# Splitting the late row blocks of a spectral-filter and GEGLU kernel into rounded halves, with three products each

## The chip, the core and the metric

The kernel runs on one core of a Trainium2 chip. A core has five engines that work in parallel, each through its own queue of instructions in a fixed order: PE (TensorE, matrix products into PSUM), ACT (ScalarE), DVE (VectorE), POOL (GpSimd) and SP (SyncE, which here only issues transfers). They wait for one another on semaphores. SBUF is the working memory, PSUM has eight banks of 128x512 floats for the products. The metric is the device time of one execution in microseconds; three runs gave 454.14, 454.15 and 454.22.

## What is computed

Two residual stages on x of 2048 rows by 512 columns, each behind a layer norm without weights (`_layernorm`): a filter in the two-dimensional Fourier domain, then a gated feed-forward.

```python
h = x + irfft2(rfft2(_layernorm(x)) * (w_r + 1j * w_i))
n = _layernorm(h)
h2 = h + (gelu(n @ w_gate) * (n @ w_up)) @ w_down
```

w_r and w_i are 2048x257, w_gate and w_up 512x1376, w_down 1376x512.

## The kernel before

The 2048 rows are 16 row blocks of 128 (row 16p + b belongs to block b, partition p). The array `gh` holds all blocks, 128x512 each, in the residual stream's place. The Fourier stages are matrix products with constant tables; the last of them, over rows, is one product per block: `mis[:, b]` (128x128) by `gh[:, b]` (128x512), into a PSUM bank. To it the input x, read again from memory into a `row` buffer, is added, and the block's mean is taken off (L972); then the block's statistics for the second norm are taken (L514, L516).

Eight blocks (0 to 7, "first half") are finished before the feed-forward starts, by a list written out by hand (`FIRST`), which fixes the order of PE, ACT, DVE and POOL. The other eight (8 to 15, the "late" blocks) are finished while the feed-forward of the first half runs, by the generator `late(b)` (L961): unfolding by four additions and subtractions on POOL (`unfolded`, L818 to L821, done within `FIRST` for blocks 8, 9 and 12, the list `BY_THEN`), then the transfer of x, the product (L971), the residual (L972) and the statistics.

The feed-forward runs over tiles (q, f): q is the half of the rows (1024 rows as 512 columns of two halves), f one of 11 column blocks of 128 of the hidden width. A tile n has seven groups P0 to P6 of two times three matmuls (a two-by-two product by seven), accumulated in three of six PSUM banks (three for even n, three for odd n). Every product of these is done in rounded precision: each operand is split into a rounded high part and the rounded rest (type F32R), and `mm3` (L100, L101, L102) adds high by high, high by low and low by high. The product at L971 is not: there both operands are full F32.

Between the groups stand copies of the bank (c1, c2, c3: L660 on ACT), additions (d1, d2, dy: L663 on DVE), the gelu (G0, G1: L666 on ACT), the multiplication (m0, m1: L669 on DVE) and the split of the result (i: L675 on ACT, o: L682 on DVE). P2 accumulates into the bank that c1 reads, P4 into the one that c2 reads, P5 into the one that c3 reads, so PE waits for these copies. The first two tiles are done in halves within `FIRST`; the last of their splits are the steps `g1bi1` and `g1bo1`.

A tile's gate and up weights come by two transfers into the one buffer `raw` (L131, L132), are combined on POOL (L138 to L146), rounded on DVE (L153, the cast) and the rest taken on POOL (L156, three instructions). The buffer `gus` of the results has two places; the cast waits until PE has done with the tile before last.

The down products (`down`, L756) of two or three finished tiles go row block by row block into banks 6 and 7 in turn (`bank_67`), and DVE adds the bank to `gh` (L762, the eviction). The late blocks' products take their bank from the same cycle. So each down waits until the bank's last user, two places before it, has been evicted. The down weights are split by L503 (ACT) and L505 (POOL).

The loop at L993 fixes PE's order alone (`manual_schedule` with PE); the scheduler orders ACT, DVE and POOL. Per tile n it calls `step(n)` (one part of the tile: P1, then P2, P3, P4, P5, P6; P0 of the next tile comes ahead of P5) and, between them, `fill(2)` (two downs). `ending` holds the late blocks of this tile: blocks 8 and 12 for n = 2, then 9 and 13 for n = 3, 10, 14, 11, 15 for n = 4 to 7. Their products stand behind P2 (`for g in ending: next(g)`, L1008).

Of the kernel before, what the change touches and what calls it, by code (L numbers as in the profile page):

```python
# [12 lines left out]
F32 = mybir.dt.float32  # L13
F32R = mybir.dt.float32r
I32 = mybir.dt.int32
AF = mybir.ActivationFunctionType
ALU = mybir.AluOpType
PSUM = bass.MemoryType.PSUM

S, D, F = 2048, 512, 1376  # L20
P = 128
# [36 lines left out]
def kernel(  # L58
# [15 lines left out]
    nc = tc.nc  # L74
    pe, act, dve, pool = nc.tensor, nc.scalar, nc.vector, nc.gpsimd
# [4 lines left out]
    gh = base.tile([P, NB, D], F32, name="gh")  # L80
# [15 lines left out]
    def mm3(o, pairs, onto=False):  # L96

        n = len(pairs)
        for i, ((lh, ll), (rh, rl)) in enumerate(pairs):
            pe.matmul(o, lh, rh, start=(i == 0 and not onto), stop=False, skip_group_check=True)  # L100
            pe.matmul(o, lh, rl, start=False, stop=False, skip_group_check=True)  # L101
            last = pe.matmul(o, ll, rh, start=False, stop=(i == n - 1), skip_group_check=True)  # L102
        return last
# [6 lines left out]
    mis = k3.tile([P, NB, P], F32, name="mis")  # L110
# [12 lines left out]
    def held(k):  # L123

        return tc.issue_after(pooled[k].ins) if k in pooled else ExitStack()
# [369 lines left out]
    w3 = ctx.enter_context(tc.tile_pool(name="w3", bufs=2, reuse_waits="tile"))  # L495
# [12 lines left out]
    def row():  # L508
        return rp.tile([P, D], F32, name="row")
# [109 lines left out]
    def products(n, i=slice(0, 4)):  # L619

        w, at = gu[tiles[n][1]], slice(i.start * P, i.stop * P)

        x, y, z = places = [ps[:, 3 * (n % 2) + k, at] for k in range(3)]

        def product(o, wm, m, onto=False):
            def do():
                mm3(
                    o,
                    [
                        (  # L630
                            (w[:, 0, wm, c], w[:, 1, wm, c]),
                            tuple(cb[:, h, m, c, i].rearrange("p i n -> p (i n)") for h in range(2)),
                        )
                        for c in range(2)
                    ],
                    onto,
                )

            return do

        return places, {
            "P0": product(x, 0, 0),
            "P1": product(y, 1, 1),
            "P2": product(x, 2, 4, True),
            "P3": product(z, 3, 3),
            "P4": product(x, 4, 5, True),
            "P5": product(x, 5, 6, True),
            "P6": product(z, 6, 2, True),
        }

    def tile_of(n, i=slice(0, 4)):

        at = slice(i.start * P, i.stop * P)
        (x, y, z), by_pe = products(n, i)
        if n not in sums:
            sums[n] = sum_tiles()
        s1, u2, u3 = (t[:, at] for t in sums[n])

        def copy(to, a):
            return lambda: act.activation(to, a, AF.Copy)  # L660

        def add(to, a, b):
            return lambda: dve.tensor_tensor(to, a, b, op=ALU.add)  # L663

        def gelu(g):
            return lambda: act.activation(g, g, AF.Gelu_apprx_tanh)  # L666

        def times(u, g):
            return lambda: dve.tensor_tensor(u, u, g, op=ALU.mult)  # L669

        def high(k, u):
            def do():
                if n not in parts_of:
                    parts_of[n] = w3.tile([P, 2, 2, 512], F32R, name="a", bufs=3)
                act.activation(parts_of[n][:, 0, k, at], u, AF.Copy)  # L675

            return do

        def low(k, u):
            def do():  # L680
                a = parts_of[n][:, :, k, at]
                dve.tensor_tensor(a[:, 1], u, a[:, 0].bitcast(F32), op=ALU.subtract)  # L682

            return do

        return by_pe | {
            "c1": copy(s1, x),
            "d1": add(s1, y, s1),
            "c2": copy(u2, x),
            "c3": copy(u3, x),  # L690
            "dy": add(y, z, u3),
            "G0": gelu(s1),
            "m0": times(x, s1),
            "i0": high(0, x),
            "o0": low(0, x),
            "d2": add(u2, z, u2),
            "G1": gelu(u2),
            "m1": times(y, u2),
            "i1": high(1, y),
            "o1": low(1, y),  # L700
        }
# [79 lines left out]
    begun_tiles, wds, parts_of, hns, copied, sums = {}, {}, {}, {}, {}, {}  # L781
    bank_67 = itertools.cycle((6, 7))

    def sum_tiles():
        return [w3.tile([P, 512], F32, name=f"s{k}") for k in range(1, 4)]
# [10 lines left out]
    do = {}  # L796
# [17 lines left out]
    def unfolded(b, v):  # L814

        s4, v4 = (a.rearrange("p (e h n) -> p e h n", e=2, h=2) for a in (gh[:, b], v))
        u = gh[:, b].rearrange("p (e n) -> p e n", e=2)
        pool.tensor_tensor(v4[:, :, 0], s4[:, :, 0], s4[:, :, 1], op=ALU.add)  # L818
        pool.tensor_tensor(v4[:, :, 1], s4[:, :, 0], s4[:, :, 1], op=ALU.subtract)
        pool.tensor_tensor(u[:, 0], v[:, :256], v[:, 256:], op=ALU.add)  # L820
        pooled["late"] = pool.tensor_tensor(u[:, 1], v[:, :256], v[:, 256:], op=ALU.subtract)  # L821
# [121 lines left out]
    def step(n):  # L943

        if n not in begun_tiles:
            f = tiles[n][1]
            if f not in gu:
                for _ in load_gu(f):
                    pass
            begun_tiles[n] = gate_up(n)  # L950
        next(begun_tiles[n])

    do["g2P0"] = lambda: step(2)
    et = mybir.EngineType
    with tc.manual_schedule(engines={et.PE, et.Activation, et.DVE, et.Pool}):
        for op in FIRST.split():
            name, *place = op.split(".")
            do[name](*map(int, place))


    def late(b):  # L961

        if b not in BY_THEN:

            with held("lo"):
                unfolded(b, row())
        yield
        xt = row()
        nc.sync.dma_start(xt, x3[:, b])
        py = ps[:, next(bank_67)]  # L970
        pe.matmul(py, mis[:, b], gh[:, b], start=True, stop=True)  # L971
        dve.scalar_tensor_tensor(gh[:, b], xt, mv[:, b, 0:1], py, op0=ALU.subtract, op1=ALU.add)  # L972
        for _ in stats2(b):
            pass
        yield

    def normed(b):

        hn = row()
        act.activation(hn, gh[:, b], AF.Copy, scale=rs2[:, b : b + 1])  # L980
        return hn

    def fill(n):
        for _ in range(n):
            next(downs, None)
# [3 lines left out]
    ending = [late(b) for b in BY_THEN[:2]]  # L989
# [3 lines left out]
    with tc.manual_schedule(engines={et.PE}):  # L993
        for n, (q, f) in list(enumerate(tiles))[2:]:
            k, at_change = n - q * NF, n == NF - 1
            if k == 0:
                step(n)
            step(n)
            if k > 8 and not q:
                for i in range(2 * k - 18, 2 * k - 16):  # L1000
                    with tc.issue_after(copied[n - 1].ins):
                        hns[i] = [normed(b) for b in (8 + i, 12 + i)]
            step(n)
            if at_change:

                steps = [in_turn(i, hns[i], banks) for i, banks in enumerate(((3, 4), (5, 0), (3, 4), (1, 2)))]
                next(steps[0])
            for g in ending:  # L1008
                next(g)
            if n in (6, 7):  # L1010

                norm_scales(2 * n - 4, 2)
            fill(2)
            step(n)
            fill(2)
            step(n)
            fill(2)

            if k == NF - 1:
                downs = down(q, orders[q][-3:], True)  # L1020
            if at_change:
                next(steps[0])
                next(steps[1])
            elif k < NF - 1:
                step(n + 1)
                fill(2)
            else:
                fill(1)
            ending = [late(b) for b in lates.get(n, ())]
            for g in ending:  # L1030
                next(g)
            step(n)
            step(n)
            if k in (4, 7):
                downs = down(q, orders[q][: k + 1][-3:], False)
            elif k == 1:
                downs = down(q, orders[q][:2], False)
            if at_change:
                gu = {f: gu[f] for f in orders[0][-2:]}
                for s in steps:  # L1040
                    for _ in s:
                        pass
                    fill(2)
            if k == NF - 1:
                fill(12)
# [125 lines left out]
```

## Time and profile before

| what | value |
|---|---|
| median of three runs | 454.15 us (454.14 to 454.22) |
| the profiled execution's own time | 454.05 us |
| its span (first to last instruction) | 452.3 us |
| mean granted PE clock | 0.998 |
| stage of the late blocks' products | 130.7 to 213 us |

The profile is one execution. A row of a timeline is start, duration, engine, line, operation, output<-inputs, sizes, count and, in brackets, how long the engine had been idle and who released it. Matmul rows overlap, since matmuls are pipelined: the distance from start to start is what one costs. A row of the chain of waits is start, length and what it was. PEld is the weight load, which runs beside PE.

### The profile page before, as it was taken

To read this page: it belongs to the slowest core of one execution; us is meant where nothing else is said; L and a number is where in the kernel's file an instruction comes from. 1 tells how busy PE (TensorE), PEld (TensorE's weight loads), DVE (VectorE), ACT (ScalarE), POOL (GpSimd) and SP (SyncE) were. 2 spreads that over 40 slices of the span, in tenths; PEclk is the share of its full clock that TensorE was granted. 3 is DMA by queue.
4 is the path that set the end of the run, shared out by engine and by line. 5 is a ranking of instruction groups with operands and counts; after the bars stand their busy time and mean duration, and the time that the engine had idled before them with its cause. 6 is when DMAs were issued, how large, how long until landed. Compare 5 with 4: busy or idle time off the path is not lost.

```text
span 452.3 us, 6433 instructions
## 1 busy us (share of the span) xinstructions
PE 437.8 (97%) x2289; PEld 371.1 (82%) x2289; DVE 277.1 (61%) x514; ACT 205.6 (45%) x433; POOL 276.5 (61%) x306
## 2 busy tenths in 40 slices
PE   3999999999999999999999999999999999999996
PEld 3999999798878777877888888888888888888875
DVE  5957895797574766358735578266555345635453
ACT  4979785688731242033332765252243034303420
POOL 6986896878859578748662543165566636653210
PEclk9999999999999999999999999999999999999999
DMA  8994805200032022112210213121022102210013
GB/s 288 390 400 147 278 13 179 100 23 1 25 116 93 26 69 93 48 46 71 70 48 23 70 48 116 49 91 46 26 70 71 46 24 71 70 46 25 23 70 118
DMA packets 21168, 41.05 MB, mean 91 GB/s; under 512 B 2064, under 2 KB 7696, under 8 KB 21008
## 3 DMA queue, kind: packets, MB, share of 16 engines
q1 hardware_dynamic: 20992, 40.51, 26.3%
q8 instruction: 18, 0.29, 0.3%
q10 hardware_dynamic: 144, 0.13, 0.1%
q14 instruction: 14, 0.11, 0.1%
HBM read 36.44 MB, written 4.19 MB: 90 GB/s over the span
## 4 chain that ended last, share of the span: by engine, by line
PE 90%; DVE 3%; ACT 2%; DMA 2%; POOL 1%; issue 1%; SPq 0%; POOLq 0%; DVEq 0%
PE ps L756 26%; PE ps L100 15%; PE ps L102 14%; PE ps L101 14%; PE ps L288 4%; PE ps L416 3%; PE ps L427 3%; PE ps L454 3%; PE ps L524 3%; PE ps L862 1%; PE ps L971 1%; DMA gh<-in_x 1%; POOL gu L156 1%; PE ps L563 1%; DMA raw<-in_wgu 1%; PE ps L557 1%
## 5 line engine op out<-in xcount | busy, mean ns | idle before, releaser
L100 PE MATMUL ps<-cb,gu 128*128 128x512 f32 (+1 forms) x336 | 127.9, 381 | 2.0 <-ACT s L660 1.6
L756 PE MATMUL ps<-wd,a 128*128 128x512 f32 (+1 forms) x537 | 125.9, 388 | 0.2 <-DVE gh L759 0.2
L102 PE MATMUL ps<-cb,gu 128*128 128x512 f32 (+1 forms) x336 | 125.0, 372 | 0.0
L101 PE MATMUL ps<-cb,gu 128*128 128x512 f32 (+1 forms) x336 | 124.9, 372 | 0.0
L756 PEld LDWEIGHTS ps<-wd,a 128*128 128x128 f32 x537 | 99.4, 188 | 21.9 <-DVE gh L972 1.0
L156 POOL TENSOR_TENSOR gu<-raw,gu 128x768 fp32r<-128x768 f32 (+1 forms) x54 | 78.3, 1479 | 39.6 <-DVE gu L153 33.4
L660 ACT ACTIVATE s<-ps 128x512 f32<-128x512 f32 (+1 forms) x72 | 40.4, 560 | 133.8 <-PE ps L102 133.5
L100 PEld LDWEIGHTS ps<-cb,gu 128*128 128x128 f32 x336 | 63.3, 188 | 14.9 <-ACT s L660 2.2
L101 PEld LDWEIGHTS ps<-cb,gu 128*128 128x128 f32 x336 | 63.3, 188 | 11.7 <-issue 1.0
L102 PEld LDWEIGHTS ps<-cb,gu 128*128 128x128 f32 x336 | 63.3, 188 | 11.0
L762 DVE TENSOR_TENSOR gh<-ps,gh 128x512 f32<-128x512 f32 x48 | 33.1, 691 | 53.7 <-PE ps L756 53.5
L505 POOL TENSOR_TENSOR wd<-wdr,wd 128x512 fp32r<-128x512 f32 x22 | 28.4, 1291 | 51.3 <-ACT wd L503 51.2
L669 DVE TENSOR_TENSOR ps<-ps,s 128x512 f32<-128x512 f32 (+1 forms) x48 | 31.0, 650 | 24.4 <-PE ps L102 22.2
L675 ACT ACTIVATE a<-ps 128x512 fp32r<-128x512 f32 (+1 forms) x48 | 26.9, 561 | 39.0 <-DVE ps L669 38.6
L682 DVE TENSOR_TENSOR a<-ps,a 128x512 fp32r<-128x512 f32 (+1 forms) x48 | 30.8, 641 | 11.5 <-ACT a L675 9.8
L663 DVE TENSOR_TENSOR s<-ps,s 128x512 f32<-128x512 f32 (+1 forms) x48 | 30.9, 643 | 10.6 <-PE ps L102 9.1
L666 ACT ACTIVATE s<-s 128x512 f32<-128x512 f32 (+1 forms) x48 | 28.2, 592 | 18.4 <-DVE s L663 18.4
L138 POOL TENSOR_TENSOR raw<-raw 128x256 f32<-128x256 f32 x20 | 14.7, 737 | 33.9 <-DMA raw<-in_wgu 32.4
L663 DVE TENSOR_TENSOR ps<-ps,s 128x512 f32<-128x512 f32 (+1 forms) x24 | 15.7, 654 | 27.8 <-ACT s L660 27.8
L288 PE MATMUL ps<-ms,pn 128*128 128x128 f32 x120 | 17.0, 291 | 7.9 <-ACT ms L256 7.8
L288 PEld LDWEIGHTS ps<-ms,pn 128*128 128x128 f32 x120 | 15.6, 205 | 8.3 <-POOL pn L263 7.2
L153 DVE CAST gu<-raw 128x1792 fp32r<-128x1792 f32 x18 | 19.6, 1091 | 3.8 <-PE ps L101 2.9
(126 smaller groups left out, 609.5 us busy)
## 6 DMA issues: line engine op xcount, KB each, us to landing
raw<-in_wgu SPq DMA_DIRECT2D x40, 256.0 KB, 3.1
wt<-in_w SPq DMA_DIRECT2D x16, 520.0 KB, 5.7
wdr<-in_wd SPq DMA_DIRECT2D x22, 256.0 KB, 2.7
out<-gh SPq DMA_DIRECT2D x15, 256.0 KB, 2.0
gh<-in_x SPq DMA_DIRECT2D x7, 512.0 KB, 8.1
row<-in_x SPq DMA_DIRECT2D x12, 256.0 KB, 3.0
mis<-in_mi SPq DMA_DIRECT2D x1, 1024.0 KB, 10.6
a<-in_x SPq DMA_DIRECT2D x4, 256.0 KB, 4.9
```

The costliest lines, as they stand in the source:

```text
L100: pe.matmul(o, lh, rh, start=(i == 0 and not onto), stop=False, skip_group_check=True)
L101: pe.matmul(o, lh, rl, start=False, stop=False, skip_group_check=True)
L102: last = pe.matmul(o, ll, rh, start=False, stop=(i == n - 1), skip_group_check=True)
L156: pooled["lo"] = pool.tensor_tensor(r[:, 1, m], t[:, m], r[:, 0, m].bitcast(F32), op=ALU.subtract)
L288: pe.matmul(pt[:, c], o, mc, start=(z == 0), stop=(z == len(parts[b][c]) - 1))
L505: pool.tensor_tensor(r[:, 1], t, r[:, 0].bitcast(F32), op=ALU.subtract)
L660: return lambda: act.activation(to, a, AF.Copy)
L663: return lambda: dve.tensor_tensor(to, a, b, op=ALU.add)
L669: return lambda: dve.tensor_tensor(u, u, g, op=ALU.mult)
L682: dve.tensor_tensor(a[:, 1], u, a[:, 0].bitcast(F32), op=ALU.subtract)
L756: pe.matmul(o, parts_of[tiles.index((q, f))][:, ha, i // 4, r], wds[f][:, hw, c], start=start, stop=stop)
L762: dve.tensor_tensor(gh[:, b, c], o, gh[:, b, c], op=ALU.add)
```

## The change

Four parts:

1. `late(b)` gets a stage of its own ahead of the product. It splits `mis[:, b]` into `m` (high and low, 128x128 each) and `gh[:, b]` into `v` (128x512 each): the high parts by a copy on ACT, the low ones by a subtraction on DVE. The product becomes `mm3`: three rounded matmuls in the place of one full-precision product. `m` and `v` have two buffers each in the pool `w3`, 2 x 5 KB per partition.
2. The splits of the first pair (8 and 12) are held behind the second tile's last split steps: ACT's copies behind `g1bi1`, DVE's subtractions behind `g1bo1`. For that, `high` and `low` return their instruction.
3. In the loop the splits of the tile's late blocks are called behind P1, the products behind P2 as before; but for n = 2 the products come behind P4.
4. The program is built with a DMA scratch of 4096 bytes (`dynamic_dma_scratch_size`), smaller than the default.

```diff
         def high(k, u):
             def do():
...
-                act.activation(parts_of[n][:, 0, k, at], u, AF.Copy)
+                return act.activation(parts_of[n][:, 0, k, at], u, AF.Copy)
...
-                dve.tensor_tensor(a[:, 1], u, a[:, 0].bitcast(F32), op=ALU.subtract)
+                return dve.tensor_tensor(a[:, 1], u, a[:, 0].bitcast(F32), op=ALU.subtract)
...
+        behind = []
         for op in FIRST.split():
             name, *place = op.split(".")
-            do[name](*map(int, place))
+            ins = do[name](*map(int, place))
+            if name in ("g1bi1", "g1bo1"):
+                behind.append(ins)
...
             with held("lo"):
                 unfolded(b, row())
+        yield
+        m = w3.tile([P, 2, P], F32R, name="m")
+        v = w3.tile([P, 2, D], F32R, name="v")
+        for h, l, full in ((v[:, 0], v[:, 1], gh[:, b]), (m[:, 0], m[:, 1], mis[:, b])):
+            with tc.issue_after(behind[0].ins) if behind else ExitStack():
+                act.activation(h, full, AF.Copy)
+            with tc.issue_after(behind[1].ins) if behind else ExitStack():
+                dve.tensor_tensor(l, full, h.bitcast(F32), op=ALU.subtract)
         yield
         xt = row()
         nc.sync.dma_start(xt, x3[:, b])
         py = ps[:, next(bank_67)]
-        pe.matmul(py, mis[:, b], gh[:, b], start=True, stop=True)
+        mm3(py, [((m[:, 0], m[:, 1]), (v[:, 0], v[:, 1]))])
...
             step(n)
+            for g in ending:
+                next(g)
+            behind = None
...
-            for g in ending:
-                next(g)
+            if n > 2:
+                for g in ending:
+                    next(g)
...
             step(n)
             fill(2)
             step(n)
+            if n == 2:
+                for g in ending:
+                    next(g)
             fill(2)
...
-    nc = bacc.Bacc("TRN2", target_bir_lowering=False, num_devices=1)
+    nc = bacc.Bacc("TRN2", target_bir_lowering=False, num_devices=1, dynamic_dma_scratch_size=4096)
```

In the text below v8 and m8 stand for the low-part subtractions of block 8 (L977 in the new file, whose copies are L975 and whose residual is L983), and so on; "down i" is the i-th down of the first group, "residual b" the instruction at L972.

## The prediction

> **What bounds the kernel now.** I read the page first (busy shares, then the chain that ended last), then the chain in order of time from 95 us, then a table of windows around the change, then each engine's timeline there.
>
> ```profile
> span 452.3 us, 6433 instructions
> PE 437.8 (97%) x2289; PEld 371.1 (82%) x2289; DVE 277.1 (61%) x514; ACT 205.6 (45%) x433; POOL 276.5 (61%) x306
> PE 90%; DVE 3%; ACT 2%; DMA 2%; POOL 1%; issue 1%; SPq 0%; POOLq 0%; DVEq 0%
> 130.70:135.60 4.90, 4.85 (x18) 2.94 (x17) 3.46 (x6) 0.60 (x1) 3.04 (x5) 1.00 0.24 86
> 135.60:153.30 17.70, 17.70 (x80) 14.66 (x79) 10.01 (x16) 3.46 (x6) 12.85 (x14) 1.00 0.19 62
> 153.30:216.00 62.70, 62.70 (x267) 49.77 (x266) 39.81 (x76) 19.33 (x35) 46.55 (x50) 1.00 0.20 63
> ```
>
> The window rows give the length, then PE, PEld, DVE, ACT, POOL busy, granted clock and DMA. All that the change touches lies between 130.7 and 216 us. There PE is never idle, at full granted clock, so a microsecond of matmul saved is a microsecond of time, and so is each one in which PE is made to wait. DVE (39.81 of 62.70) and ACT (19.33) have room on average; POOL is busy for 12.85 of 17.70 and 46.55 of 62.70.
>
> **The products: what they cost and will cost.**
>
> ```profile
> 132.64 3.05 PE ps L756 x12
> 137.06 2.72 PE ps L756 x12
> 153.38 1.72 PE ps L971 x4
> 164.67 0.86 PE ps L971 x2
> 155.17 0.40 PE L101 MATMUL ps<-cb,gu 128*128 128x512 f32 x1
> 157.03 0.39 PE L100 MATMUL ps<-cb,gu 128*128 128x512 f32 x1
> ```
>
> The first four rows are of the chain, in order of time. A full-precision product is two passes, 0.86 us for one block; 12 rounded matmuls take 2.72, so three take 0.68. Removed: 8 x 0.86 = 6.88; added: 8 x 0.68 = 5.44; saved 1.44. After each full-precision product the next rounded matmuls come slower: from 155.17 to 157.03 are eight in 1.86, 0.2325 apiece against 0.227, 0.05 per place. Five places follow the first one; I count four, 0.20 (bounds 0 and 0.25). The first pair also stalls: 12 products of L756 take 3.05 instead of 2.72, 0.33, and with 0.04 between product and start the loss is 0.37. The first pair moves behind the second tile's P4, so this goes too. Gains: 1.44 + 0.20 + 0.37 = 2.01 us.
>
> **The splits: ACT.** Per block a copy of 128x512 and one of 128x128.
>
> ```profile
> 129.57 1.08 ACT L811 ACTIVATE gh<-ps 128x512 f32<-128x512 f32 x2
> 141.67 0.62 ACT L503 ACTIVATE wd<-wdr 128x512 fp32r<-128x512 f32 x1
> 142.19 0.62 ACT L666 ACTIVATE s<-s 128x512 f32<-128x512 f32 x1
> L489 ACT ACTIVATE nis<-mis 128x128 f32<-128x128 f32 x2 | 0.5, 300 | 0.0
> ```
>
> 0.62 us each, the next 0.52 later; 0.30 for the small one. In the built program the first pair's four stand behind the two copies that end at 130.65; they end near 132.1 and push the copy c2 of tile 2 from 130.97 to 132.0. PE first needs c2 for P4, and between lie 12 products, P3 (1.36) and 12 products more: 137.5. I cost them at nothing; without this cover it would be 1.0 us. The later copies stand where ACT idles.
>
> **The splits: DVE, and the port it shares with POOL.** Each of the 16 new subtractions (L977) reads two SBUF operands. After 130 us no DVE subtraction or addition here does: one operand is always in PSUM. At the start of the kernel some do.
>
> ```profile
> 28.52 0.42 DVE L275 TENSOR_TENSOR us<-pn 128x256 f32<-128x256 f32 x1
> L762 DVE TENSOR_TENSOR gh<-ps,gh 128x512 f32<-128x512 f32 x48 | 33.1, 691 | 53.7 <-PE ps L756 53.5
> 14.30 1.55 DVE L277 TENSOR_TENSOR uv<-pn 128x512 f32<-128x512 f32 x1
> 14.03 1.27 POOL L263 TENSOR_TENSOR pn<-gh 128x512 f32<-128x512 f32 x1
> 15.26 1.73 POOL L262 TENSOR_TENSOR pn<-gh 128x512 f32<-128x512 f32 x1
> 72.93 0.73 DVE L444 TENSOR_TENSOR z<-z 128x2 f32<-128x2 f32 x1
> 72.90 0.73 POOL L441 TENSOR_TENSOR z<-t,t 128x260 f32<-128x260 f32 x1
> ```
>
> Alone, 256 elements take 0.42 and 512 some 0.69. But the one at 14.30 lasts 1.55: POOL's operation ends at 15.30, DVE's 0.55 to 0.59 later, and POOL's next lasts 1.73 instead of 1.27. Two elements at 72.93 take 0.73, as long as the POOL operation beside them. So they exclude one another, and a waiting engine comes in between two operations of the other. I use: 512 elements end 0.57 after the POOL operation they wait for, 128 elements 0.17 after; a POOL operation of 0.73 that waited ends 0.60 after DVE's. Alone, the small one is taken as 0.29, between the rows above and nothing.
>
> By the Trainium skill (SBUF — State Buffer, section "SBUF: two separate sides") that pair of ports is an exclusive lock, held for the whole instruction by whichever of a GpSimd operation and a DVE operation with two SBUF inputs starts first. The 1.55 agrees; that rule speaks against this change.
>
> **First pair, walked through** on the time axis of before, with the built program's queues (DVE: v8, m8, v12, eviction of down 0, m12, eviction 1, the cast, evictions 2 and 3, residual 8, dy, residual 12, statistics, v9, m9, m13, statistics, eviction 4).
>
> ```profile
> 131.12 0.73 POOL L138 TENSOR_TENSOR raw<-raw 128x256 f32<-128x256 f32 x1 [3.60 <-DMA raw<-in_wgu]
> 131.84 0.75 DVE L972 SCALAR_TENSOR_TENSOR gh<-row,mv,ps 128x512 f32<-128x512 f32 x1 [1.28 <-POOL raw L138]
> 135.33 0.69 DVE L514 BATCH_NORM_STATS2 bn<-gh 128x6 f32<-128x512 f32 x1
> 135.49 4.35 POOL L156 TENSOR_TENSOR gu<-raw,gu 128x256 fp32r<-128x256 f32 x3 [1.21 <-DVE gu L153]
> 136.90 2.88 PE L756 MATMUL ps<-wd,a 128*128 128x512 f32 x12
> 138.46 0.69 DVE L762 TENSOR_TENSOR gh<-ps,gh 128x512 f32<-128x512 f32 x1 [1.17 <-PE ps L756]
> 139.80 0.75 POOL L818 TENSOR_TENSOR row<-gh 128x256 f32<-128x256 f32 x1
> 142.73 1.28 POOL L505 TENSOR_TENSOR wd<-wdr,wd 128x512 fp32r<-128x512 f32 x1
> 147.78 0.39 PE L100 MATMUL ps<-cb,gu 128*128 128x512 f32 x1
> ```
>
> A down's eviction can start 1.56 after the down (138.46 - 136.90); DVE instructions follow 0.60 apart. Down 0 starts at 130.72, down 1 at 132.08, P3 at 133.44; down 2 wants bank 6 at 134.81. v8 meets L138 and ends at 131.85 + 0.57 = 132.42; POOL 133.02; m8 133.19; POOL 133.84; v12 134.41; eviction 0 135.01. First stall 0.25. Then P4 ends at 139.14, the two products at 139.82 and 140.50; residual 8 holds bank 6 from 140.02 to 140.77, and down 4 starts at 140.82: second stall 0.32 (before, the same wait cost part of the 0.37). P0 of the next tile ends at 144.90, where down 6 wants bank 6 again, and ahead of eviction 4 stand dy, residual 12, statistics, v9, m9, m13, statistics. POOL runs without a gap from the end of the cast at 136.78: L156 to 141.15, L818, L819 to 142.55, L505, L820. v9, issued at 142.53, ends at 143.12; POOL's L505 144.28; m9 144.45; L820 145.05; m13 145.20; statistics 145.8; eviction 4 146.40: third stall 1.55. Down 7 ends at 149.17 against 147.78: this place loses 0.25 + 0.32 + 1.55 - 0.37 - 0.36 = 1.39 us.
>
> Bounds of the third stall: without waiting for the port eviction 4 ends at 144.6, no stall; if L505 gets the port ahead of v9 (they ask within 0.03 us), 2.25. I take 1.55, since POOL's L819 ends just as v9 asks. First stall: 0 to 0.5.
>
> **Block 14.** The other blocks find their splits done early; not this one.
>
> ```profile
> 173.39 0.75 POOL L821 TENSOR_TENSOR gh<-row 128x256 f32<-128x256 f32 x1
> 174.09 0.74 POOL L138 TENSOR_TENSOR raw<-raw 128x256 f32<-128x256 f32 x1
> 174.94 1.02 PE L971 MATMUL ps<-gh,mis 128*128 128x512 f32 x2
> ```
>
> POOL finishes the block at 174.14, 0.80 ahead of its product. Now copy (0.62 and 0.05 to start) and subtraction (0.69) come between. POOL's chain there hangs on PE through the cast and comes some 0.34 earlier; PE reaches the product 0.59 earlier, at 174.35. Copy 173.85 to 174.47, subtraction to 175.25, so the second matmul waits: 0.67. Bounds: 0, were POOL a further 0.7 earlier, and 1.24, if L138 or its successor gets the port first.
>
> **The rest at nothing.** SP's queue keeps its order and its waits, POOL's queue two neighbour exchanges (the low half of wd ahead of an unfolding). The smaller DMA scratch removes no transfer; the page has no issue on POOL's queue that would fill it, and DMA is 0.20 busy. If it delayed every weight load by 0.5 us, that would still be covered where it is tightest, at tile 5:
>
> ```profile
> 165.72 4.36 POOL L156 TENSOR_TENSOR gu<-raw,gu 128x256 fp32r<-128x256 f32 x3 [1.41 <-DVE gu L153]
> 168.13 0.39 PE L100 MATMUL ps<-cb,gu 128*128 128x512 f32 x1
> ```
>
> The first of the three weight parts is done 0.74 after 165.72, 1.7 us before PE takes it. So 0; with that cover gone it would be what exceeds 1.7 us.
>
> Sum: -2.01 + 0.25 + 0.32 + 1.55 + 0.67 = +0.78 us. The profiled execution took 454.05, 1.75 outside its span and 0.10 under the median, so **454.8 us**: no change that a measurement of this kernel can tell, for which I take 0.2%, 0.9 us.
>
> **The rivals.**
>
> 1. The port costs little: DVE's small subtractions keep it back to back, or POOL is elsewhere. Stalls of 0.32 and some 0.5 at block 14 remain: -2.01 + 0.82 = -1.2, **452.8**. For it: DVE is idle for a third of the stage. Against: each two-operand DVE operation near POOL's in the trace waited.
> 2. Slower: POOL wins the port ahead of v9 and at block 14, and eviction 4 is late by 2.25, the product by 1.24: -2.01 + 0.25 + 0.32 + 2.25 + 1.24 = +2.05, **456.1**. It decides from the point where eviction 4 ends after 146.1, 1.2 us behind the end of P0. For it: L505 and v9 ask at the same moment.
> 3. The change doesn't do what it says: three passes with three weight loads cost no less than two. Then 1.64 of gain is gone and the waits stay: 456.5. Against: 0.227 for every L756 and L100 to L102.
>
> **How the numbers follow.** Forecast 0.40, rivals 0.33, 0.22 and 0.05. The forecast's own range is 453.9 to 455.6; 0.28 of its 0.40 lie within 0.9 us of 454.15 and 0.12 above. Rival 1 gives 0.31 faster, 0.02 same; rival 2 0.02 same, 0.20 slower; rival 3 all slower. So faster 0.31, same 0.32, slower 0.37. With every stall at nothing the time would be 452.0, with the upper bounds 456.3; the range 452.4 to 456.2 leaves out little of either end.
>
> **What would show it.** Right: L977 of 512 elements lasting over 1 us where POOL is busy; L756 waiting for DVE L762 once near 145 us by more than 1 us, and the L101 of block 14 waiting for DVE; three matmuls of a block 0.68 us apart from start to next start. Wrong: PE without gaps from 135 to 150 us (rival 1), L977 always 0.69; or a wait at some third place, such as PE waiting for the copies c1 to c3, in front of which ACT now has more work.

## The result and the profile after

| | before | after |
|---|---|---|
| median of ten runs, same chip | 454.19 us (453.93 to 454.60) | 455.10 us (454.99 to 455.61) |
| the profiled execution | 454.05 us | 455.29 us |
| its span | 452.3 us | 453.5 us |

The ratio of after to before is 1.0022, with a 95% interval of 1.0013 to 1.0031: slower, by 0.9 us, about as much as was taken for the least that can be told from no change. The forecast was 454.8 us. The kernels below are compared by such ratios to before; each has an interval of 0.1 to 0.2% to either side.

The page of the changed kernel, first its totals and then the shares of the chain that ended last:

```profile
span 453.5 us, 6476 instructions
PE 437.7 (97%) x2297; PEld 373.2 (82%) x2297; DVE 288.7 (64%) x530; ACT 211.7 (47%) x449; POOL 279.9 (62%) x306
PE 82%; POOL 9%; issue 3%; ACT 2%; DVE 2%; DMA 2%; SPq 0%; POOLq 0%; DVEq 0%
```

PE's busy time is within 0.1 us of before, its idle time 1.3 us more (453.5 - 437.7 = 15.8 against 452.3 - 437.8 = 14.5). POOL's share of the chain rose from 1% to 9%: the chain of after runs from block 14's wait back over POOL's queue to 122 us. That is no lost time by itself, since PE works beside it, but it says that PE now waits at the end of POOL's work. Where PE idles, the table of windows shows (length, then PE, PEld, DVE, ACT, POOL busy, clock, DMA share, GB/s); in before PE was idle for 0.05 us between 130.7 and 216 us:

```profile
130.70:135.60 4.90, 4.90 (x23) 4.04 (x23) 3.56 (x7) 2.14 (x6) 3.64 (x4) 1.00 0.30 107
135.60:155.00 19.40, 17.90 (x78) 14.15 (x77) 15.21 (x24) 4.91 (x10) 13.95 (x15) 1.00 0.17 56
155.00:217.00 62.00, 61.75 (x271) 50.40 (x270) 45.54 (x80) 22.61 (x42) 47.50 (x49) 1.00 0.20 64
```

PE is idle for 1.50 us in the second window and 0.25 in the third, at a full granted clock. The view of waits names what PE's matmuls waited for from 120 us on (total, times, longest):

```profile
PE ps L756 <- DVE gh L762: 1.3, 1, 1.3
...
PE ps L101 <- DVE v L977: 0.2, 1, 0.2
...
PE ps L756 <- DVE gh L983: 0.2, 1, 0.2
```

One wait for an eviction, one for a low part, one for a residual: the places of the prediction's third stall, of block 14 and of its second stall. The first and the last are in the timeline of the changed kernel, PE, DVE and POOL in order of time:

```profile
131.46 0.69 DVE L977 TENSOR_TENSOR v<-gh,v 128x512 fp32r<-128x512 f32 x1 [0.64 <-ACT v L975]
131.72 1.02 POOL L138 TENSOR_TENSOR raw<-raw 128x256 f32<-128x256 f32 x1 [3.95 <-DMA raw<-in_wgu]
132.07 0.82 DVE L977 TENSOR_TENSOR m<-mis,m 128x128 fp32r<-128x128 f32 x1
...
133.42 0.68 DVE L762 TENSOR_TENSOR gh<-ps,gh 128x512 f32<-128x512 f32 x1
134.02 0.28 DVE L977 TENSOR_TENSOR m<-mis,m 128x128 fp32r<-128x128 f32 x1
...
140.02 0.75 DVE L983 SCALAR_TENSOR_TENSOR gh<-row,mv,ps 128x512 f32<-128x512 f32 x1 [1.35 <-PE ps L102]
140.83 3.04 PE L756 MATMUL ps<-wd,a 128*128 128x512 f32 x12 [0.16 <-DVE gh L983]
...
142.55 0.72 DVE L977 TENSOR_TENSOR v<-gh,v 128x512 fp32r<-128x512 f32 x1
142.66 1.75 POOL L505 TENSOR_TENSOR wd<-wdr,wd 128x512 fp32r<-128x512 f32 x1
143.19 2.12 DVE L977 TENSOR_TENSOR m<-mis,m 128x128 fp32r<-128x128 f32 x2
143.70 0.39 PE L100 MATMUL ps<-cb,gu 128*128 128x512 f32 x1
144.37 0.78 POOL L820 TENSOR_TENSOR gh<-row 128x256 f32<-128x256 f32 x1
144.84 0.39 PE L102 MATMUL ps<-cb,gu 128*128 128x512 f32 x1
145.23 0.68 DVE L514 BATCH_NORM_STATS2 bn<-gh 128x6 f32<-128x512 f32 x1
145.84 0.67 DVE L762 TENSOR_TENSOR gh<-ps,gh 128x512 f32<-128x512 f32 x1
146.56 3.04 PE L756 MATMUL ps<-wd,a 128*128 128x512 f32 x12 [1.34 <-DVE gh L762]
149.44 0.39 PE L100 MATMUL ps<-cb,gu 128*128 128x512 f32 x1
```

A duration here holds the wait for the port, as that of the row at 14.30 in the prediction did. Two subtractions of 128x128 (m9 and m13) take 2.12 us beside L505 and L820, where one at 134.02 takes 0.28. Eviction 4 stands behind them and ends at 146.51, and down 6 starts at 146.56, 1.49 after P0's end (144.84 + 0.23).

Set side by side, the starts at the same points of PE's work give the lag of after over before:

| point on PE | before | after | lag |
|---|---|---|---|
| behind P2 of tile 2 (next: product 8 before, down 0 after) | 130.72 | 130.98 | 0.26 |
| P5 behind down 7 | 147.78 | 149.44 | 1.66 |
| product 10 | 164.51 | 165.86 | 1.35 |
| where product 14 could start | 174.94 | 176.07 (175.84 + 0.23) | 1.13 |
| downs behind product 14 | 175.80 (174.94 + 0.86) | 177.55 | 1.75 |
| product 11 | 201.68 | 203.40 | 1.72 |
| a group behind product 15 | 222.53 | 223.80 | 1.27 |

The 0.26 at the head lies ahead of the new work. Six of the kernels below do the same work up to there and stand at 130.65 to 131.09, and the kernel before with the smaller scratch alone stands at 130.75, so executions differ by that much by themselves. From this head on, the first place costs 1.40 on balance, block 14 costs 0.80 less the saving of its product, and the products of the other blocks give back about 0.2 each (0.31 for 9 and 13 together).

### The profile page after: what moved, and what is told of

Read it like the earlier page. It is cut to its first block, busy times and chain, and to the rows that moved or that the text cites. A ratio compares the mean times of both kernels' runs of the same rounds, so it can differ in the third digit from the quotient of the medians.

```text
span 453.5 us, 6476 instructions
## 1 busy us (share of the span) xinstructions
PE 437.7 (97%) x2297; PEld 373.2 (82%) x2297; DVE 288.7 (64%) x530; ACT 211.7 (47%) x449; POOL 279.9 (62%) x306
## 4 chain that ended last, share of the span: by engine, by line
PE 82%; POOL 9%; issue 3%; ACT 2%; DVE 2%; DMA 2%; SPq 0%; POOLq 0%; DVEq 0%
PE ps L756 24%; PE ps L100 12%; PE ps L101 12%; PE ps L102 12%; PE ps L288 5%; POOL gu L156 3%; PE ps L416 3%; PE ps L427 3%; PE ps L454 3%; PE ps L524 3%; PE ps L862 1%; POOL wd L505 1%; DMA gh<-in_x 1%; PE ps L563 1%; DMA raw<-in_wgu 1%
## 5 line engine op out<-in xcount | busy, mean ns | idle before, releaser
L156 POOL TENSOR_TENSOR gu<-raw,gu 128x768 fp32r<-128x768 f32 (+1 forms) x54 | 78.4, 1480 | 38.7 <-DVE gu L153 38.7
L505 POOL TENSOR_TENSOR wd<-wdr,wd 128x512 fp32r<-128x512 f32 x22 | 28.9, 1313 | 50.5 <-ACT wd L503 50.4
L138 POOL TENSOR_TENSOR raw<-raw 128x256 f32<-128x256 f32 x20 | 15.5, 775 | 33.4 <-DMA raw<-in_wgu 32.3
L288 PEld LDWEIGHTS ps<-ms,pn 128*128 128x128 f32 x120 | 16.6, 216 | 7.5 <-POOL pn L263 7.5
```

Source lines behind the costliest of these rows:

```text
L156: pooled["lo"] = pool.tensor_tensor(r[:, 1, m], t[:, m], r[:, 0, m].bitcast(F32), op=ALU.subtract)
L288: pe.matmul(pt[:, c], o, mc, start=(z == 0), stop=(z == len(parts[b][c]) - 1))
L505: pool.tensor_tensor(r[:, 1], t, r[:, 0].bitcast(F32), op=ALU.subtract)
```

## The experiments

There are eight runs, e_pool to e_where. Each is timed against the kernel before on the same chip, whose median was 454.24 us for e_pool, e_evict, e_products and e_scratch (22 runs) and 454.41 us for the others (15 runs).

### The port: POOL's work taken out of the stretch

In the changed kernel (run e_pool) the third down weight's low half on POOL (L505) and the first step of the unfolding of block 13 are made to wait for eviction 5. DVE's order up to there stays as it is. `evicted` holds the evictions in their order; the lines that fill it are left out here and in the next run.

```diff
-        pool.tensor_tensor(r[:, 1], t, r[:, 0].bitcast(F32), op=ALU.subtract)
+        i = pool.tensor_tensor(r[:, 1], t, r[:, 0].bitcast(F32), op=ALU.subtract)
+        if f == 2 and len(evicted) == 8:
+            wait_for(i, evicted[5])
...
-        pool.tensor_tensor(v4[:, :, 0], s4[:, :, 0], s4[:, :, 1], op=ALU.add)
+        i = pool.tensor_tensor(v4[:, :, 0], s4[:, :, 0], s4[:, :, 1], op=ALU.add)
+        if b == 13:
+            wait_for(i, evicted[5])
...
```

> The changed kernel with POOL kept away from the stretch in which DVE does the low parts of blocks 9 and 13: the low half of the third down weight and the unfolding of block 13 wait for the eviction of down 5. DVE's queue up to eviction 4 is that of the changed kernel. Port theory (the small subtractions waited for POOL): the two low parts of m take 0.28 us each instead of 2.12 together, eviction 4 ends about 1.6 us earlier and PE's wait of 1.34 us before down 6 goes; time 455.1 - 1.5 = 453.6. Rival, the queue alone (statistics and five more instructions ahead of eviction 4 make it late whatever POOL does): wait unchanged, 455.1.

Measured: 457.84 us, ratio 1.0095 (1.0079 to 1.0112). Neither theory's time. The timeline of this kernel (lines were added, so L987 is the former L977, L770 the eviction, L764 the down, L826 the first step of the unfolding):

```profile
142.48 0.68 DVE L987 TENSOR_TENSOR v<-gh,v 128x512 fp32r<-128x512 f32 x1
143.07 0.49 DVE L987 TENSOR_TENSOR m<-mis,m 128x128 fp32r<-128x128 f32 x2
...
144.08 0.68 DVE L770 TENSOR_TENSOR gh<-ps,gh 128x512 f32<-128x512 f32 x1
144.97 2.91 PE L764 MATMUL ps<-wd,a 128*128 128x512 f32 x12
145.50 0.74 POOL L826 TENSOR_TENSOR row<-gh 128x256 f32<-128x256 f32 x1 [3.56 <-DVE mv L524]
147.72 0.39 PE L100 MATMUL ps<-cb,gu 128*128 128x512 f32 x1
...
176.79 0.72 POOL L831 TENSOR_TENSOR gh<-row 128x256 f32<-128x256 f32 x1
178.32 0.50 PE L100 MATMUL ps<-v,m 128*128 128x512 f32 x1 [1.75 <-ACT v L985]
```

With POOL idle the same two subtractions take 0.49 instead of 2.12, eviction 4 ends at 144.76, and down 6 starts without a wait; P5 stands at 147.72 (149.44 in after). So POOL's work beside them is what made them long, and the order on DVE alone does not cause the stall. But POOL sat idle for 3.56 us, and it does not catch up: it finishes block 14 at 177.51 (in after at 175.53), PE waits 1.75 and then 0.79 there, and for shorter times elsewhere (0.78 at 160.90 for the addition dy, 0.40 at 165.90). A wait taken from DVE was put on POOL, whose slack in this stage is less. What I had left out of both expectations is that later price.

### The port: DVE's work taken out of the stretch

The same collision taken away from the other side (run e_evict): the low parts of blocks 9 and 13 come behind eviction 7; POOL's queue stays.

```diff
-            with tc.issue_after(behind[1].ins) if behind else ExitStack():
+            with tc.issue_after(behind[1].ins if behind else evicted[7].ins) if behind or b in (9, 13) else ExitStack():
```

> The changed kernel with DVE's low parts of blocks 9 and 13 held behind the eviction of down 7. Both theories: eviction 4 is free at once and the third stall (1.50 and 0.16 us to start again) goes: 455.1 - 1.7 = 453.4. If the lost time lay elsewhere (in ACT's copies, in the scratch), 455.1. If the low parts then come too late for the products of 9 and 13, a new wait there and 454 to 455.

Measured: 453.65 us, ratio 0.9987 (0.9978 to 0.9996). From its timeline:

```profile
142.41 1.30 POOL L505 TENSOR_TENSOR wd<-wdr,wd 128x512 fp32r<-128x512 f32 x1
142.89 0.68 DVE L762 TENSOR_TENSOR gh<-ps,gh 128x512 f32<-128x512 f32 x1
144.81 2.88 PE L756 MATMUL ps<-wd,a 128*128 128x512 f32 x12
147.53 0.39 PE L100 MATMUL ps<-cb,gu 128*128 128x512 f32 x1
148.34 1.04 DVE L978 TENSOR_TENSOR v<-gh,v 128x512 fp32r<-128x512 f32 x1
...
160.20 0.50 PE L100 MATMUL ps<-cb,gu 128*128 128x512 f32 x1 [0.27 <-DVE ps L663]
```

L505 takes 1.30 where after had 1.75, eviction 4 ends at 143.57, and the stall is gone. From down 0 to P5 are 16.80 us (147.53 - 130.73) against 18.46 in after: 1.66 less, and the ratio is 0.35% below that of after, 1.6 us. v9 now waits for POOL instead (1.04), where PE needs nothing of what is queued behind it.

The trace does not keep the whole 1.66. At 160.20 PE waits for dy: on DVE's queue that addition stands behind the next low part of `m`, which lasts 1.61 from 154.96 on, beside POOL's L156, and DVE has no gap from there to dy. From down 0 to product 10 are 33.72 us against 34.88, so 1.16 is left there, and 1.18 at the group behind product 15. The ratios can't tell 1.2 from 1.6. So by the order of the queue the same collision comes a second time, some 12 us later, which the prediction did not price; no run takes that one away.

### Block 14

Product 14 comes behind P4 of its tile, as the first pair's do, and nothing else changes (run e_14).

```diff
-            if n > 2:
+            if n not in (2, 5):
...
-            if n == 2:
+            if n in (2, 5):
```

> The changed kernel with block 14's product behind P4 of its tile instead of behind P2, some 9 us later. Theory (its split comes too late, because POOL finishes the block just ahead): the wait of 0.8 us goes, 455.1 - 0.8 = 454.3. Rival (the wait moves on to the next eviction or to the statistics): 455.1.

Measured: 454.15 us, ratio 0.9997 (0.9988 to 1.0006): 0.25% below after, 1.1 us; from down 0 to the group behind product 15 its trace is 0.90 shorter. What it removes is this, in the timeline of the changed kernel:

```profile
174.80 0.73 POOL L821 TENSOR_TENSOR gh<-row 128x256 f32<-128x256 f32 x1
175.50 0.73 POOL L138 TENSOR_TENSOR raw<-raw 128x256 f32<-128x256 f32 x1
175.56 0.63 ACT L975 ACTIVATE v<-gh 128x512 fp32r<-128x512 f32 x1 [0.67 <-POOL gh L821]
175.84 0.39 PE L102 MATMUL ps<-cb,gu 128*128 128x512 f32 x1
176.23 0.69 DVE L977 TENSOR_TENSOR v<-gh,v 128x512 fp32r<-128x512 f32 x1
176.25 0.50 PE L100 MATMUL ps<-v,m 128*128 128x512 f32 x1
176.98 0.50 PE L101 MATMUL ps<-v,m 128*128 128x512 f32 x1 [0.22 <-DVE v L977]
```

POOL ends at 175.53, the copy at 176.19, the subtraction at 176.92. The three matmuls could start at 176.07 and be done by 176.75; the next work starts at 177.55, so 0.80 is lost. The subtraction takes 0.69, its time alone: L138 had left the port at 176.23. This stall is the two steps put in series behind a POOL that was already close, not the port. With product 14 moved, PE's one long wait in this stage is that for eviction 4 (1.4 us).

### Both at once

> Both repairs: the low parts of 9 and 13 held behind the eviction of down 7, and block 14's product behind P4. If the two waits are independent: 455.1 - 1.7 - 0.8 = 452.6, faster than the kernel before (454.2) by 1.6 us. If one hid the other: 453.4 to 454.3.

Run e_both has e_evict's and e_14's edits together: 452.64 us, ratio 0.9966 (0.9952 to 0.9979). It beats both kernels. Its waits of PE from 120 to 300 us, of which the first two stand in before as well:

```profile
PE ps L100 <- ACT s L660: 0.5, 1, 0.5
PE ps L100 <- DVE ps L663: 0.3, 1, 0.3
PE ps L756 <- DVE gh L984: 0.2, 1, 0.2
```

Against after the ratio is lower by 0.56%, 2.5 us; the two stalls of the trace are 1.66 + 0.80 = 2.46, and from down 0 to the group behind product 15 it takes 90.42 against 92.82, 2.40 less. What is left of the losses is residual 8's place (0.32 and its restart) and about 0.2 near 160 us.

### The last stall as well

On top of e_both (run e_all), the first pair's products are set apart, product 8 behind P3 and product 12 behind P4, so that down 4 need not wait for residual 8.

```diff
+            if n == 2:
+                next(ending[0])
             fill(2)
...
-                for g in ending:
-                    next(g)
+                next(ending[1])
+            if n == 5:
+                next(ending[0])
```

> As with both repairs, and the first pair's products apart: block 8 behind P3, block 12 behind P4 of tile 2, so that each residual has a down's 1.36 us to free its bank. The wait of 0.33 and the second one of 0.15 us should go: 452.6 - 0.5 = 452.1. If evictions then come late instead, 452.6 or more.

Measured: 452.94 us, ratio 0.9967 (0.9954 to 0.9979): no gain over e_both. The timeline of this kernel:

```profile
135.45 1.09 DVE L153 CAST gu<-raw 128x1792 fp32r<-128x1792 f32 x1 [0.87 <-POOL raw L146]
136.46 0.74 DVE L984 SCALAR_TENSOR_TENSOR gh<-row,mv,ps 128x512 f32<-128x512 f32 x1
137.26 1.67 PE L756 MATMUL ps<-wd,a 128*128 128x512 f32 x6 [0.33 <-DVE gh L984]
```

Product 8 is done before the cast ends, and residual 8 stands behind the cast on DVE's queue. The cast waits for POOL's L146 and runs 1.09 us, and a down waits for the residual as before. The expected gain went into a wait at the neighbouring place.

### The products alone

In the kernel before (run e_products), each L971 becomes three rounded matmuls on operands that are ready anyway, with no copy and no subtraction; the last row transform of the late blocks is left out of the result.

```diff
-        pe.matmul(py, mis[:, b], gh[:, b], start=True, stop=True)
+        mm3(py, [((cb[:, 0, 0, 0, 0], cb[:, 1, 0, 0, 0]), tuple(cb[:, h, 0, 0].rearrange("p i n -> p (i n)") for h in range(2)))])
```

> The kernel before with three rounded matmuls in the place of each full-precision product, on operands that lie ready (pieces of the tile input), so without any split; the late blocks' back transform is left out of the result. It prices the products alone: six blocks by 0.18 us, while the first pair behind P2 gains nothing, since down 0 then waits longer for the residual: 454.2 - 1.1 = 453.1. If the matmuls behind a full-precision product also get faster, 452.8. If three rounded matmuls cost as much as one full-precision product, 454.2.

Measured: 452.77 us, 1.47 under before; ratio 0.9969 (0.9956 to 0.9981). The interval is too wide to say what it is made of, but the starts in the two traces say it:

| point on PE | before | e_products | gained since the last point |
|---|---|---|---|
| behind P2 of tile 2 | 130.72 | 130.86 | |
| P5 behind down 7 | 147.78 | 147.71 | 0.21 |
| product 10 | 164.51 | 164.03 | 0.41 |
| product 14 | 174.94 | 174.23 | 0.23 |
| product 11 | 201.68 | 200.75 | 0.22 |
| a group behind product 15 | 222.53 | 221.15 | 0.45 |

The six products behind the first pair gain 1.31: 6 x 0.18 = 1.08 for themselves and 0.23 for their faster neighbours. The first pair gains 0.21, where I had expected nothing. That the total of 1.47 is also 8 x 0.18 is chance.

### The scratch alone

The kernel before with part 4 of the change alone (run e_scratch).

```diff
-    nc = bacc.Bacc("TRN2", target_bir_lowering=False, num_devices=1)
+    nc = bacc.Bacc("TRN2", target_bir_lowering=False, num_devices=1, dynamic_dma_scratch_size=4096)
```

> The kernel before with the DMA scratch of 4096 bytes alone. Predicted cost nothing: 454.2. Rival: the 0.26 us that the changed kernel's profile is late at 130 us, ahead of all other parts of the change, come from the scratch: 454.5.

Measured: 454.32 us, ratio 1.0004 (0.9995 to 1.0012). It costs nothing that can be told, as expected, and its first late product starts at 130.75, 0.03 behind before, so it does not explain the 0.26 of the head.

### The first pair where it was

The changed kernel, but with the first pair's products behind P2 as in before (run e_where); a single execution.

```diff
-            if n > 2:
+            if n > 1:
...
-            if n == 2:
+            if n == 0:
```

> The changed kernel with the first pair's products behind P2, as before the change. The splits of 8 and 12 end at 134 us in the changed kernel's profile and P2 at 131: PE should wait about 2 us for v and m of block 8, and the residuals then hold the banks as before: 455.1 + 1 to 3 = 456 to 458. If the splits could be had sooner, 455.1.

Measured: 459.50 us (span 457.7). Two lines of its timeline:

```profile
131.80 0.50 PE L100 MATMUL ps<-v,m 128*128 128x512 f32 x1 [0.55 <-ACT m L975]
138.28 1.65 PE L756 MATMUL ps<-wd,a 128*128 128x512 f32 x6 [1.55 <-DVE gh L983]
```

PE now waits for the halves themselves and later for a residual behind the cast; the time is above what I put on it. One execution says that the later place is needed, not to a tenth how much it is worth.

## Why the prediction was right

The forecast time is 0.3 us low, and three of its four stalls came where they were put. Its words "no change that a measurement of this kernel can tell" were a little too strong: the interval of ten runs, 1.0013 to 1.0031, lies above 1. Step by step, in the order of the prediction:

- **What bounds.** PE without idle time, so every wait counts in full. Held: a lag in the table above stays until a cheaper product gives some of it back.
- **Products, 1.44, and faster neighbours, 0.20.** Six products lie behind the first pair. Their gains in the lag table are 0.31 for 9 and 13 together, 0.22 for 10, 0.18 reckoned for 14, 0.03 more up to product 11, 0.45 for 11 and 15: 1.19, where 6 x 0.18 is 1.08. So 0.18 apiece held. The neighbours are worth the 0.20 (0.23 in e_products), but after shows only 0.11 on balance: from 161.68 to 164.50 twelve rounded matmuls take 2.82 instead of 2.72. They begin at the product that waits for dy in e_evict; that dy is what slows them in after is likely, not shown.
- **ACT's copies, SP, the scratch at nothing.** PE waits for no copy c1 to c3 at the first pair, and e_scratch measured the scratch by itself.
- **Stall 1, 0.25: did not occur.** I let L138 hold the port when v8 came. In the run v8 was there first (131.46 against 131.72), since its copy was done before the transfer that L138 waits for. That was close: in the seven traces with these splits v8 is ahead by 0.04 to 0.26. In after L138 took 1.02 instead of 0.73, and eviction 0 ended at 134.10, 0.96 ahead of down 2. What the other order would cost was not tried.
- **Stall 2, 0.32: 0.32 and 0.15.** Product 12 is done at 140.51 (140.28 + 0.23), residual 8 at 140.77, and down 4 starts at 140.83. That these clock times are the predicted ones is luck: the walk was on the time axis of before and had a first stall of 0.25 in them, which did not occur, while after was 0.26 late from the head. The twelve matmuls behind the gap take 2.87 instead of 2.72. I had not priced that restart, though the 3.05 in the prediction's first rows held one: those twelve start at 132.64 and the next group at 135.53, 2.89.
- **Stall 3, 1.55: 1.49 and 0.16.** The walk (v9, L505, m9, L820, m13, statistics, eviction 4) is what the rows show, in that order, with v9 0.11 ahead of L505. The sign that I gave for it came otherwise: of the eight subtractions of 512 elements one lasted over 1 us (1.27 at 210.40, where it cost nothing), and at this place the wait was in those of 128. e_pool and e_evict each take one side of the collision away, and with it the stall. By the rule of the Trainium skill (SBUF — State Buffer, section "SBUF: two separate sides") that the first to start keeps the port for its whole instruction, L505 should be longer by what v9 has left: 142.66 to 143.27 is 0.61 and the row has 0.45 more than its 1.30 alone, so the trace agrees to 0.16.
- **The first place together, 1.39: 1.40.** That agreement is better than the steps deserve: a stall of 0.25 that did not occur stands against two restarts of 0.15 and 0.16 that were not priced. So that part of the agreement is luck.
- **Block 14, 0.67: 0.80.** PE reached the block 0.54 after POOL ended it (0.55 in the prediction), and the wait for the subtraction is 0.68 as priced; the 0.12 beside it is again the restart.
- **The sum.** From the head, after is 1.40 + 0.80 - 1.19 = 1.01 us behind, predicted 0.78; with 0.26 that lay ahead of the change that is the 1.24 between the two profiled executions, to 0.03.

Of the rivals, the first (the port costs little, 452.8) fell with the 2.12 us of m9 and m13, though its time is nearly that of e_both, where the collision is scheduled away. The second (POOL wins the port, 456.1) fell with v9 ahead of L505; it was decided by 0.11 us, and no run shows the other order. The third (three passes cost as much as two) fell with e_products.

## What to carry to other kernels

Where DVE and POOL can exclude one another, price a small DVE instruction with two SBUF inputs by the POOL instruction beside it, not by its size, and look at what stands behind it on DVE's queue: here an eviction that PE needs. The cure was to move the small instructions behind that eviction; alone it gave back about 0.5 of the 1.66 at a later place, together with block 14's repair about 0.2. Holding back POOL instead, which has less slack there, cost more later than the stall had. When two more steps are put in front of a product, compare their length with the slack between the product and its last input, block by block: one of eight had too little.

## What the runs showed that was not expected

**A restart costs PE about 0.15 us beyond the wait.** After a gap the first matmul lasts 0.50 instead of 0.39, and twelve take 2.87 (140.83 to 143.70) and 2.88 (146.56 to 149.44) instead of 2.72. In e_products, behind a wait of 0.23, they take 2.86 (132.61 to 135.47).

**The granted clock fell behind a stretch of waits.** In the profiled execution of e_pool the windows around product 14 (columns as above) read:

```profile
176.40:179.80 3.40, 0.86 (x3) 0.38 (x3) 1.91 (x3) 1.60 (x3) 3.24 (x5) 1.00 0.50 157
179.80:183.40 3.60, 3.60 (x10) 2.78 (x10) 2.64 (x5) 0.31 (x1) 1.22 (x3) 0.53 0.02 5
183.40:186.80 3.40, 3.40 (x17) 2.80 (x16) 1.38 (x2) 0.00 (x0) 3.40 (x3) 1.00 0.00 0
```

PE was busy for 0.86 of 3.40 us, and then ran 3.6 us at a mean clock of 0.53: 10 matmuls where the next 3.4 us have 17. Shorter windows show 0.91 from 179.50 to 180.00, 0.50 from 180 to 183 and 0.84 from 183 to 184, from which I estimate a half clock from 179.9 to 183.3, 3.4 us. The 18 matmuls of the next group and the group behind them take 6.84 us (180.38 to 187.22) where after has 5.45 (177.55 to 183.00), 1.39 more. This execution took 459.52; the median of five, 457.84, is 1.7 less. The Trainium skill (TensorE: Matmul & The Clock Gate, section "What's actually happening") has the clock halved after an idle window of about 3.4 us. This trace agrees on the half and on the length, as far as one event can: PE's dense work ended at 176.41 (176.18 + 0.23), 3.5 us ahead of the drop. But PE was not idle in between, it was busy for a quarter of the time. That the sparse stretch brought the drop about is likely, not tested. The stall of 1.34 us in after did not do this: its clock stayed at 1.00.
